# Second FFN stage: 20 products in another order, other stored weight sums, weights by order of use, and more of its start made ready in the first stage

## The chip, the cores and the metric

The kernel runs on one core of a Trainium2 chip. The metric is the device time of one execution in microseconds, from several runs; lower is better. One further execution was recorded by the profiler, and the profile and the trace come from it. The engines in them are PE (TensorE, matmuls), PEld (its weight loads), DVE (VectorE), ACT (ScalarE), POOL (GpSimd) and SP (SyncE, which here issues nearly all DMAs).

## The reference

Attention with a sigmoid in place of the softmax, for 8 batches of 12 heads, 448 positions and head size 64, then a feed-forward network with a leaky ReLU on all 3584 tokens (768 to 2048 to 768 features):

```python
scores = scale * np.matmul(q, k.transpose(0, 1, 3, 2)) - np.log(S)
attn = 1.0 / (1.0 + np.exp(-scores))
attn_out = np.matmul(attn, v)
x = attn_out.transpose(0, 2, 1, 3).reshape(B * S, H * D)
h = x @ w_in
g = np.maximum(0.01 * h, h)
out = g @ w_out
```

The values are float32 on the way in and out; the weights come as float64.

## The kernel before

**Precision.** A float32 operand is split into a high part, rounded by ScalarE (a cast), and a low part, the rest, subtracted by VectorE. A product of two such operands is three matmuls: high by high, high by low, low by high (`parts_mm`, L188, and the list at L976).

**Three stages.** First the attention. Beside it VectorE turns the float64 weights into float32 and makes the sums of weight blocks that the later stages use (`prep`, L342, with `firsts` and `second`); blocks and sums go to HBM. Then comes the first FFN stage (`First`, L629). It works on 4 quarters of the tokens (two batches of 448 each), and in each on 8 steps u with 7 products (a fast scheme for a 2 x 2 by 2 x 2 block product), a product being 9 matmuls of 128 x 448. Each u gives four blocks of g after the leaky ReLU. They are stored in HBM (`gd`), and so are sums of two of them that are named in `MADE` (L39), so that the second stage needn't make them.

**The second FFN stage.** In a quarter `w_out` is a grid of 3 x 4 blocks and g one of 4 x 2 blocks; the out grid has 3 x 2. Instead of 24 block products the kernel makes 20 (`PRODUCTS`, L42). A row of that table is: the weight form (a block or a sum of blocks, numbered by its place in HBM), the chain (A to E, an accumulator of two PSUM banks that goes on over several products), the operand ("21-30" is g block 21 less g block 30), and the reads of the accumulator that follow. "c10" copies the accumulator into output block 10 (ScalarE); "r", "+" and "-" combine it with a block already begun (VectorE: accumulator less block, block plus accumulator, block less accumulator); "!" says that the block is then complete, and it is stored. In the listing, products are counted from 0 in the order of the table.

A product has two halves, h = 0 and 1, each with half of the inner dimension. One half of one product is an item: 12 matmuls. There are 160 items, `items` (L787), 40 in each quarter. An item's operand is one of two kinds. If it lies in HBM as such (a raw block or a sum from `MADE`) it is one load, a cast and a subtraction. If not, two blocks are loaded, unless the product before has one of them, and VectorE first makes the sum, the tile gf (`Operand`, L800, steps `load`, `whole`, `high`, `low`).

All these tiles and the output blocks being built come from one list of 18 free buffers (12 in `gp`, 6 in `op`), first in, first out (`grab`, `drop`). A buffer goes back to the list when the instruction that ends its use has been issued; whoever gets it next waits on the chip until that use is over. The 6 of `op` join the list when the first FFN stage has been issued.

**The order of the work.** Every engine does its instructions in the order in which the program lists them; this order is written out by hand. In item k (`work`, L964) the program lists: the sum for item k+2 (for k+3 if it shares a block with a product that is itself a single load), the low part of k+1, the high part of k+2, the steps of the weight tiles that are due, the reads of the product that ended with item k-1 (L971), the 12 matmuls, the release of the item's operand, and then the loads (`g_load`, L881) of as many of the next items, up to 8 ahead, as the free list allows after the buffers that the next steps want (`wanted`, L869). A store is listed one item after the read that completes a block. All loads and stores go through SP, which waits at each of them until its buffer is free.

**Weights of the second stage.** 20 forms in 7 groups (`TRIPLES`, three forms each, the last with two) by 4 quarters of the inner dimension make 28 tiles (`Wide`, L165), each loaded, cast and split once. The first `AHEAD` = 7 of them are made ready in the last quarter of the first FFN stage (loop at L895, one every 6 products), the others during the first quarter of the second stage, one every 1.5 items. The same loop lists the first loads and steps of items 0 to 2 in the last five products of the first stage.

**Weights of the first stage.** They are staged, cast and split three and two products ahead (`advance`, L610), and in the last quarter a pool of 4 more staging buffers (L784) is there.

Of the kernel before, what the change touches and what calls it, by code (L numbers as in the profile page):

```python
# [25 lines left out]
AHEAD = 7  # L26
GG, OO, FAR = 12, 6, 8
# [11 lines left out]
MADE = {"01+30": "01", "00+30": "00", "10-21": "10", "21-20": "21", "11-10": "11", "11-21": "11"}  # L39
# [8 lines left out]
BLOCKS = "02", "01", "10", "00", "21", "03", "22", "11", "12", "13", "20", "23"  # L48
# [19 lines left out]
def attn_ffn_kernel(ctx: ExitStack, tc: tile.TileContext, qk, v, w_in, w_out, out):  # L68
# [245 lines left out]
    def second(u, dec):  # L314


        to = t2d[u // 2][:, u % 2]
        w = dec.rearrange("p a b -> p (a b)").rearrange("p (n m) -> p n m", m=P)
        dma(out=to[:, 7:8], in_=w[:, 0:1])
        dma(out=to[:, 10:17], in_=w[:, 1:8])  # L320
        s = block(F32, (12, P), f"ws1_{u}")

        def two(x, i, j):
            end = j + (1 if j > i else -1)
            return x[:, i:end if end >= 0 else None:j - i]

        def at(x, y):
            return two(w, BLOCKS.index(x), BLOCKS.index(y))

        for fn, to_, x, y in (  # L330
                (add, two(s, 8, 9), at("02", "03"), at("12", "13")), (sub, two(s, 10, 11), at("00", "03"), at("20", "23")),
                (sub, two(s, 1, 2), two(s, 9, 11), at("10", "22")), (add, two(s, 5, 6), two(s, 8, 10), at("11", "21")),
                (sub, two(s, 0, 4), at("10", "20"), at("13", "21")), (sub, two(s, 0, 4), two(s, 0, 4), two(s, 2, 1)),
                (sub, two(s, 3, 7), at("11", "01"), two(s, 2, 6)), (add, s[:, 3], s[:, 3], w[:, BLOCKS.index("12")]),
                (add, s[:, 7], s[:, 7], s[:, 5])):
            fn(to_, x, y)
            yield
        dma(out=to[:, :7], in_=s[:, :7])
        dma(out=to[:, 8:10], in_=s[:, 7:9])
        dma(out=to[:, 17:], in_=s[:, 9:])  # L340
# [443 lines left out]
    more = ExitStack()  # L784
    w1_stage.extend([more.enter_context(tc.tile_pool(name="stage2", bufs=4, side="right", reuse_waits="tile"))])
# [14 lines left out]
    class Operand:  # L800
# [4 lines left out]
        def __init__(self, k):  # L805
# [9 lines left out]
            self.lent, self.made, self.hi, self.ready = (), None, None, False  # L815
# [34 lines left out]
        def high(self):  # L850
            if self.hi is None:
                self.hi = grab(self.label("gh"))
            copy(out=self.hi, in_=self.x)

        def low(self):
            sub(self.lo, self.x, self.hi)
            if self.made is not None:
                drop(self.made)
# [10 lines left out]
    def wanted(k):  # L869
# [24 lines left out]

    for k in range(NOP, size):  # L895
        m, at = divmod(k - NOP, 6)
        if m < AHEAD:
            x = w2[use[m]]
            if at == 1:
                later(0, x.load)  # L900
                later(3, x.high)
                later(4, x.low)
        rest = size - k
        if rest <= 5:
            later(0, lambda r=rest: g_load(-r, 5 - r))
        for at, what in {2: ((0, "whole"), (0, "high")), 1: ((2, "whole"), (1, "whole"), (0, "low"), (1, "high"))}.get(rest, ()):
            later(0, lambda at=at, what=what: g_step(at, what))
        slot(first.step)
    while chores:
        slot()  # L910
    ps.close()
    more.close()
# [10 lines left out]
    psum = banks("ps_o", dict(acc=(4, 2)))  # L923
    firsts_at = {}
    for i, (_, chain, _, _) in enumerate(PRODUCTS):
        firsts_at.setdefault(chain, i)
    outs, accs = {}, {}
# [11 lines left out]
    def read(p, i):  # L939
        _, chain, _, reads = PRODUCTS[i]  # L940
        acc = accs[p, chain][:, :, :S]
        for x in reads:
# [8 lines left out]
            if x[3:]:  # L951
                later(1, lambda o=o: store(p, o))

    loads = {}
    for j in range(len(use) - AHEAD):
        loads.setdefault(j * 3 // 2, []).append(w2[use[AHEAD + j]])

    for k, (p, i, h) in enumerate(items):
        form, chain, _, reads = PRODUCTS[i]
        begins = h == 0 and firsts_at[chain] == i  # L960
        if begins:
            accs[p, chain] = psum("acc", f"acc{p}_{chain}")
        ending = k == len(items) - 1
        def work():  # L964
# [6 lines left out]
            if k % 2 == 0 and k:  # L971
                read(*items[k - 1][:2])
            me = operands[k]
            g = form // 3
            for m in range(2):
# [4 lines left out]
                if ending:  # L980
# [3 lines left out]
                    for cols, queue in zip(HALVES, (dma, dma_act)):  # L984
                        add(t[:, m, cols], t[:, m, cols], acc[:, m, cols])
# [51 lines left out]
```

## Time and profile before

| | |
|---|---|
| median of 3 runs | 1082.77 us (1082.52 to 1086.28) |
| profiled execution | 1081.94 us |
| its span, first to last instruction | 1080.1 us |
| mean granted TensorE clock | 0.993 |
| DMA bytes | 294.95 MB, 273 GB/s over the span |
| second FFN stage, first to last matmul | 658.46 to 1076.5 us |

How to read the rows: in a list of waits the numbers are microseconds in total, times, and the longest. A timeline row has start, duration, engine, line, operation, tiles and count, and in brackets the idle time before it with what ended it. A row of the chain has start, length, and engine or DMA. A group row has the busy time, the mean duration of one in ns, and the idle time before with what ended most of it. A DMA row has the KB of one transfer and the median from issue to landing. Nearly all instructions are issued through one helper, so they all have line 103, and the tile names tell them apart: px, py and pz are the first stage's accumulators, acc_A to acc_E those of the second; g is a loaded block (and later the low part), gf a sum made at run time, gh a high part, o an output block, w a weight tile, wx its staging tile.

### The profile page before, as it was taken

The numbers are of one execution on the slowest core, as the hardware profiler recorded it, in microseconds if no ns is written. First come the engines' busy times: TensorE is split into PE (matmuls) and PEld (weight loads), VectorE is DVE, ScalarE is ACT, GpSimd is POOL, SyncE is SP. The second block draws the span as 40 slices with busy tenths as digits, with TensorE's granted clock in tenths as the row PEclk, the third lists the DMA queues.
The fourth block names the chain that finished last, engine by engine and source line by source line (L and its number), as shares of the span: only waits on it lengthen the run. The fifth ranks groups of instructions, "written<-read, shape, count | busy, mean of one in ns | idle before, by whom it ended". The sixth has DMA issues, their size and how long they took to land.

```text
span 1080.1 us, 16340 instructions
## 1 busy us (share of the span) xinstructions
PE 1052.3 (97%) x5786; PEld 874.3 (81%) x5786; DVE 827.7 (77%) x1187; ACT 608.0 (56%) x829; POOL 0.3 (0%) x5
## 2 busy tenths in 40 slices
PE   9999999999999999999999999998999999999997
PEld 5555555558999998999899998987998899889977
DVE  5778889777897898789766566988767866786586
ACT  6877878876656655655565555754543344334432
POOL 0000000000000000000000000000000000000000
PEclk9999999999999999999999999999999999999999
DMA  7888888897889888998888789978946885697574
GB/s 260 275 289 274 288 296 271 278 330 224 269 264 334 258 279 265 301 338 277 284 246 272 251 277 363 356 266 307 341 157 222 304 315 194 196 339 266 188 249 159
DMA packets 126849, 294.95 MB, mean 273 GB/s; under 512 B 13360, under 2 KB 66608, under 8 KB 126768
## 3 DMA queue, kind: packets, MB, share of 16 engines
q1 hardware_dynamic: 126048, 293.23, 80.3%
q8 instruction: 45, 0.74, 0.3%
q10 hardware_dynamic: 720, 0.69, 0.2%
q14 instruction: 36, 0.29, 0.1%
HBM read 207.22 MB, written 86.64 MB: 272 GB/s over the span
## 4 chain that ended last, share of the span: by engine, by line
PE 80%; DVE 8%; DMA 8%; issue 2%; SPq 0%; ACT 0%; DVEq 0%; ACTq 0%
PE px_h L103 19%; PE pv L103 12%; PE sc L103 11%; PE acc_A L103 10%; PE pz_h L103 10%; PE acc_B L103 9%; PE py_h L103 5%; DMA out<-o 4%; DMA g<-g 3%; PE acc_C L103 3%; DVE g L103 2%; PE acc_D L103 2%; DVE gf L103 2%; DVE o L103 1%; DVE w L103 1%
## 5 line engine op out<-in xcount | busy, mean ns | idle before, releaser
L103 PE MATMUL px_h<-hi,w 128*128 128x448 f32 x768 | 231.8, 362 | 3.0 <-DVE w L103 3.0
L103 PEld LDWEIGHTS px_h<-hi,w 128*128 128x128 f32 x768 | 143.3, 187 | 16.3 <-DVE w L103 5.6
L103 PE MATMUL px_h<-lo,w 128*128 128x448 f32 x384 | 139.4, 363 | 0.0
L103 ACT ACTIVATE s<-sc 128x896 f32<-128x896 f32 x144 | 119.4, 933 | 9.4 <-PE sc L103 9.4
L103 ACT CAST gh<-gf 128x896 fp32r<-128x896 f32 x64 | 60.3, 942 | 112.0 <-DVE gf L103 100.4
L103 PE MATMUL pz_h<-hi,w 128*128 128x448 f32 x384 | 117.9, 361 | 0.0
L103 DVE TENSOR_TENSOR gf<-g,g 128x896 f32<-128x896 f32 x80 | 87.1, 1089 | 37.5 <-PE acc_A L103 16.1
L103 DVE TENSOR_TENSOR g<-g,gh 128x896 fp32r<-128x896 f32 x80 | 86.5, 1089 | 36.9 <-ACT gh L103 35.4
L103 DVE TENSOR_TENSOR w<-wx,w 128x768 fp32r<-128x768 f32 (+1 forms) x128 | 109.1, 853 | 6.2 <-ACT w L103 6.2
L103 PE MATMUL pv<-s,v 128*64 128x448 f32 x576 | 113.8, 543 | 0.0
L103 PE MATMUL acc_B<-gh,w 128*128 128x448 f32 x384 | 112.1, 362 | 0.0
L103 ACT CAST gh<-g 128x896 fp32r<-128x896 f32 x80 | 74.9, 942 | 54.5 <-PE acc_B L103 22.2
L103 PEld LDWEIGHTS sc<-qks 64*128 64x128 f32 x876 | 80.2, 188 | 23.8 <-issue 16.9
L103 ACT CAST w<-wx 128x768 fp32r<-128x768 f32 (+1 forms) x128 | 95.9, 750 | 0.7 <-DMA wx<-t 0.7
L103 PE MATMUL sc<-qks 64*128 64x448 f32 (+1 forms) x876 | 95.8, 369 | 0.2 <-ACT qks L103 0.2
L103 PE MATMUL acc_A<-gh,w 128*128 128x448 f32 x320 | 93.4, 362 | 0.0
L103 PEld LDWEIGHTS pv<-s,v 128*64 128x64 f32 x576 | 39.1, 137 | 63.3 <-issue 53.8
L103 ACT COPY c_h<-px_h 128x448 f32<-128x448 f32 x64 | 34.1, 533 | 89.5 <-PE px_h L103 80.3
L103 PE MATMUL acc_A<-g,w 128*128 128x448 f32 x256 | 78.1, 362 | 2.6 <-DVE g L103 2.6
L103 PEld LDWEIGHTS pz_h<-hi,w 128*128 128x128 f32 x384 | 71.9, 187 | 5.1
L103 PEld LDWEIGHTS acc_B<-gh,w 128*128 128x128 f32 x384 | 72.0, 187 | 4.9
L103 DVE TENSOR_TENSOR g<-gf,gh 128x896 fp32r<-128x896 f32 x64 | 69.4, 1086 | 8.5 <-ACT gh L103 8.5
(75 smaller groups left out, 1782.2 us busy)
## 6 DMA issues: line engine op xcount, KB each, us to landing
g<-g SPq DMA_DIRECT2D x200, 448.0 KB, 4.9
wx<-t SPq DMA_DIRECT2D x96, 384.0 KB, 4.5
g<-c_h SPq DMA_DIRECT2D x128, 224.0 KB, 4.5
g<-s SPq DMA_DIRECT2D x96, 224.0 KB, 4.5
qk<-in_qk SPq DMA_DIRECT2D x46, 448.0 KB, 5.3
wr<-in_w_in SPq DMA_DIRECT2D x32, 384.0 KB, 3.3
wr<-in_w_out SPq DMA_DIRECT2D x32, 384.0 KB, 3.8
out<-o SPq DMA_DIRECT2D x23, 448.0 KB, 5.1
```

What stands on the lines that cost most here:

```text
L103: return lambda *args, **kw: tc.keep_in_program_order(issue(*args, **kw))
```

## The change

- `PRODUCTS` has the same 20 kinds of products in another order, with other chains, and some sums have changed. `MADE` holds three other sums: 01-00, 20-10 and 31+01 in place of 00+30, 10-21 and 11-21. It is now a plain list.
- The weight forms lie in HBM in a new order (`FORM`), near the order of use; `second` writes them in seven pieces instead of five.
- The accumulators are four named pairs of banks, given out from a list that a chain joins again when its last read has been listed.
- `wanted` keeps two more buffers back (`SPARE`).
- Nine weight tiles (`AHEAD`) instead of seven are made ready in the first stage, one every 5 products, and those left are loaded one every 1.75 items. The four extra staging buffers are given up for the space.
- Items 0 to 3 are made ready wholly in the first stage, items 4 and 5 up to their sums, one step per product, ending two products before the stage's end (`READY`, `LEAD`).
- `advance` makes the first stage's weights ready one product earlier.
- The last read may add or subtract.

```diff
-AHEAD = 7
-GG, OO, FAR = 12, 6, 8
+AHEAD = 9
+GG, OO, FAR, SPARE = 12, 6, 8, 2
+READY, LEAD = 4, 2
...
-MADE = {"01+30": "01", "00+30": "00", "10-21": "10", "21-20": "21", "11-10": "11", "11-21": "11"}
+MADE = ("01+30", "01-00", "11-10", "20-10", "21-20", "31+01")
...
 PRODUCTS = (
-    (0, "A", "30", ("c10",)), (2, "B", "21-30", ("c21",)), (1, "A", "01+30", ("c11",)), (3, "B", "21", ("r11",)),
-    (4, "A", "01", ("r21",)), (5, "B", "10-21", ("c01",)), (6, "A", "10+01", ("c20",)), (7, "B", "21-20", ("c00",)),
-    (8, "A", "10", ("r00",)), (9, "B", "20-10", ()), (10, "A", "11-10", ("r01",)), (11, "B", "00+30", ("r10!",)),
-    (12, "D", "01-00", ("-00!",)), (13, "E", "11+01", ()), (14, "C", "30-31", ("-01!", "-21")), (15, "D", "30-20", ()),
-    (17, "C", "31+01", ()), (19, "E", "21-31", ("+21!",)), (18, "D", "10+00", ("-20!",)), (16, "C", "11-21", ("+11!",)))
-BLOCKS = "02", "01", "10", "00", "21", "03", "22", "11", "12", "13", "20", "23"
+    (0, "E", "11+01", ()), (1, "A", "30", ("c10",)), (2, "B", "21-30", ("c21",)), (3, "A", "01+30", ("c11",)),
+    (4, "E", "21-31", ("r21",)), (5, "C", "30-31", ("-21", "c01")), (7, "A", "01", ("+21!",)), (8, "B", "21", ("r11",)),
+    (6, "D", "01-00", ("c00",)), (9, "B", "10-21", ("+01",)), (10, "A", "10+01", ("c20",)), (11, "B", "21-20", ("+00",)),
+    (13, "A", "10", ("r00!",)), (12, "D", "30-20", ()), (14, "B", "20-10", ()), (15, "C", "31+01", ()),
+    (16, "D", "10+00", ("-20!",)), (17, "C", "11-21", ("+11!",)), (18, "B", "00+30", ("r10!",)), (19, "A", "11-10", ("r01!",)))
+FORM = ("21", "s0", "s2", "s1", "s11", "03", "00", "s4", "s3", "s5", "s6", "02", "22", "s7", "s8", "s9", "s10", "11", "10", "01")
+SUMS = tuple(x for x in FORM if x[0] == "s")
+BLOCKS = (*(x for x in FORM if x not in SUMS), "12", "13", "20", "23")
...
-        dma(out=to[:, 7:8], in_=w[:, 0:1])
-        dma(out=to[:, 10:17], in_=w[:, 1:8])
+        def keep(x, names, raw):
+            at = 0
+            for raw_, run in itertools.groupby(FORM, key=lambda name: name not in SUMS):
+                run = list(run)
+                if raw_ == raw:
+                    i = names.index(run[0])
+                    dma(out=to[:, at:at + len(run)], in_=x[:, i:i + len(run)])
+                at += len(run)
+
+        keep(w, BLOCKS, True)
...
-        while at_high < len(w1) and w1[at_high][0] <= t + 3:
+        while at_high < len(w1) and w1[at_high][0] <= t + 3 + (t >= 7):
...
-        while at_low < len(w1) and w1[at_low][0] <= t + 2:
+        while at_low < len(w1) and w1[at_low][0] <= t + 2 + (t >= 7):
...
-    w1_stage.extend([more.enter_context(tc.tile_pool(name="stage2", bufs=4, side="right", reuse_waits="tile"))])
...
         n += x.single or len([m for m in x.new if m not in x.lent]) < 2
+        n += SPARE
...
+    todo = []
+    for k in range(READY):
+        todo.append((k, "load"))
+    for k in range(READY):
+        todo += [(k + 2, "load")] * (k + 2 >= READY) + [(k, "whole"), (k, "high")]
+        todo += [(k + 2, "whole")] * bool(operands[k + 2].first()) + [(k, "low")]
+    ahead = READY + 2
+
     for k in range(NOP, size):
-        m, at = divmod(k - NOP, 6)
+        m, at = divmod(k - NOP, 5)
         if m < AHEAD:
             x = w2[use[m]]
-            if at == 1:
-                later(0, x.load)
-                later(3, x.high)
-                later(4, x.low)
-        rest = size - k
-        if rest <= 5:
-            later(0, lambda r=rest: g_load(-r, 5 - r))
-        for at, what in {2: ((0, "whole"), (0, "high")), 1: ((2, "whole"), (1, "whole"), (0, "low"), (1, "high"))}.get(rest, ()):
-            later(0, lambda at=at, what=what: g_step(at, what))
+            for n, what in ((0, "load"), (2, "high"), (3, "low")):
+                if at == n:
+                    later(0, getattr(x, what))
+        if k >= size - LEAD - len(todo) and todo:
+            later(0, lambda x=todo.pop(0): g_step(*x))
         slot(first.step)
...
-    psum = banks("ps_o", dict(acc=(4, 2)))
-    firsts_at = {}
+    psum = banks("ps_o", {f"acc{n}": (1, 2) for n in range(4)})
+    vacant, held = [3, 0, 1, 2], {}
+    firsts_at, lasts_at = {}, {}
...
+        if i == lasts_at[chain]:
+            vacant.append(held.pop((p, chain)))
...
-        loads.setdefault(j * 3 // 2, []).append(w2[use[AHEAD + j]])
+        loads.setdefault(j * 7 // 4, []).append(w2[use[AHEAD + j]])
...
+            if begins:
+                held[p, chain] = vacant.pop(0)
+                accs[p, chain] = psum(f"acc{held[p, chain]}", f"acc_{chain}{p}")
...
-                        add(t[:, m, cols], t[:, m, cols], acc[:, m, cols])
+                        x, y = (t, acc) if reads[0][0] in "+-" else (acc, t)
+                        (add if reads[0][0] == "+" else sub)(t[:, m, cols], x[:, m, cols], y[:, m, cols])
```

`high` and `low` of an operand now return at once if they were done before.

More of the change, by code (lines that the diff above doesn't have):

```diff
@@ L1 @@
+import itertools
 import math
@@ L328, in at, with sums, one @@
             return two(w, BLOCKS.index(x), BLOCKS.index(y))
+        def sums(i, j):
+            return two(s, SUMS.index(f"s{i}"), SUMS.index(f"s{j}"))
+        def one(i):
+            return s[:, SUMS.index(f"s{i}")]
         for fn, to_, x, y in (
[L331 to L335, printed above, removed]
+                (add, sums(8, 9), at("02", "03"), at("12", "13")), (sub, sums(10, 11), at("00", "03"), at("20", "23")),
+                (sub, sums(1, 2), sums(9, 11), at("10", "22")), (add, sums(5, 6), sums(8, 10), at("11", "21")),
+                (sub, sums(0, 4), at("10", "20"), at("13", "21")), (sub, sums(0, 4), sums(0, 4), sums(2, 1)),
+                (sub, sums(3, 7), at("11", "01"), sums(2, 6)), (add, one(3), one(3), w[:, BLOCKS.index("12")]),
+                (add, one(7), one(7), one(5))):
             fn(to_, x, y)
             yield
-        dma(out=to[:, :7], in_=s[:, :7])
-        dma(out=to[:, 8:10], in_=s[:, 7:9])
-        dma(out=to[:, 17:], in_=s[:, 9:])
+        keep(s, SUMS, False)
     def prep():
@@ L814, in __init__ @@
             self.new = [n for n in self.names if n not in self.shared]
-            self.lent, self.made, self.hi, self.ready = (), None, None, False
+            self.lent, self.made, self.hi = (), None, None
+            self.ready = self.has_high = self.has_low = False
             if self.before:
@@ L850, in high @@
         def high(self):
+            if self.has_high:
+                return
+            self.has_high = True
             if self.hi is None:
@@ L855, in low @@
         def low(self):
+            if self.has_low:
+                return
+            self.has_low = True
             sub(self.lo, self.x, self.hi)
@@ L893, in attn_ffn_kernel @@
     w2 = {(g, u): Wide(g, u, t2a, "t2") for g, u in use[:AHEAD]}
+    todo = []
[5 more added lines that the diff above has]
+    ahead = READY + 2
     for k in range(NOP, size):
-        m, at = divmod(k - NOP, 6)
+        m, at = divmod(k - NOP, 5)
         if m < AHEAD:
             x = w2[use[m]]
-            if at == 1:
-                later(0, x.load)
-                later(3, x.high)
-                later(4, x.low)
-        rest = size - k
-        if rest <= 5:
-            later(0, lambda r=rest: g_load(-r, 5 - r))
-        for at, what in {2: ((0, "whole"), (0, "high")), 1: ((2, "whole"), (1, "whole"), (0, "low"), (1, "high"))}.get(rest, ()):
-            later(0, lambda at=at, what=what: g_step(at, what))
+            for n, what in ((0, "load"), (2, "high"), (3, "low")):
[3 more added lines that the diff above has]
+            later(0, lambda x=todo.pop(0): g_step(*x))
         slot(first.step)
+    assert not todo
     while chores:
@@ L911, in attn_ffn_kernel @@
     ps.close()
-    more.close()
     left.close()
@@ L922, in attn_ffn_kernel @@
         w2[g, u] = Wide(g, u, pool, tag, KQ if small else None)
-    psum = banks("ps_o", dict(acc=(4, 2)))
-    firsts_at = {}
+    psum = banks("ps_o", {f"acc{n}": (1, 2) for n in range(4)})
+    vacant, held = [3, 0, 1, 2], {}
+    firsts_at, lasts_at = {}, {}
     for i, (_, chain, _, _) in enumerate(PRODUCTS):
         firsts_at.setdefault(chain, i)
+        lasts_at[chain] = i
     outs, accs = {}, {}
@@ L960, in attn_ffn_kernel @@
         begins = h == 0 and firsts_at[chain] == i
-        if begins:
-            accs[p, chain] = psum("acc", f"acc{p}_{chain}")
         ending = k == len(items) - 1
```

1 line of the change is left out of this document (removed).

## The prediction

> **What bounds the kernel now.** I read the page's engine line first, then PE's waits by stage, then the chain that ended last, then the timeline of one stall.
>
> ```profile
> PE 1052.3 (97%) x5786; PEld 874.3 (81%) x5786; DVE 827.7 (77%) x1187; ACT 608.0 (56%) x829; POOL 0.3 (0%) x5
> ...
> PE px_h L103 <- DVE w L103: 3.0, 6, 1.3
> ...
> PE acc_C L103 <- DVE g L103: 12.7, 9, 2.2
> PE acc_A L103 <- DVE g L103: 2.6, 2, 1.6
> PE acc_C L103 <- DVE o L103: 1.0, 2, 0.8
> ```
>
> TensorE is the bound, and no matmul is removed, so only what it loses can be won. The waits are few and have one form: it wants an operand (g) that VectorE hasn't finished; the 3.0 us on w are in the first FFN stage. But they don't give the whole loss; the timeline does.
>
> ```profile
> 658.46 0.37 PE L103 MATMUL acc_A<-gh,w 128*128 128x448 f32 x1
> 659.82 0.47 PE L103 MATMUL acc_A<-g,w 128*128 128x448 f32 x1 [0.99 <-DVE g L103]
> 664.09 0.47 PE L103 MATMUL acc_A<-g,w 128*128 128x448 f32 x1 [1.59 <-DVE g L103]
> ...
> 767.65 4.80 PE acc_A L103 x24
> 869.77 4.80 PE acc_A L103 x24
> 972.55 4.80 PE acc_A L103 x24
> ...
> 1075.02 0.47 PE L103 MATMUL acc_C<-gh,w 128*128 128x448 f32 x1 [0.78 <-DVE o L103]
> 1076.13 0.37 PE L103 MATMUL acc_C<-gh,w 128*128 128x448 f32 x1
> ```
>
> A product (counted from 0) is 24 matmuls in 4.80 us, 0.20 each; an item, its half, is 2.4. The stage has 4 quarters of 20 products, 1920 matmuls, 384.0 us. It runs from 658.46 to 1076.13 + 0.2: 417.9 us, so **33.9 us are lost**. The quarters begin at 658.46, 767.65, 869.77 and 972.55 (the chain counts from 0.16 inside) and take 109, 102.1, 102.8 and 103.9 where 96.0 would do. The start rows cost 0.99 + 1.59, and about 0.28 more each for the pipe (below): 3.1. The last wait costs 0.78 + 0.28 = 1.06. The other 29.7 lie late in the quarters; here is the stall of the second one.
>
> ```profile
> 835.54 0.37 PE L103 MATMUL acc_C<-gh,w 128*128 128x448 f32 x1
> 838.01 0.47 PE L103 MATMUL acc_C<-g,w 128*128 128x448 f32 x1 [2.10 <-DVE g L103]
> ...
> 839.79 0.95 PE L103 MATMUL acc_C<-gh,w 128*128 128x448 f32 x2
> 840.54 0.58 PE L103 MATMUL acc_C<-g,w 128*128 128x448 f32 x1
> ...
> 833.08 1.08 DVE L103 TENSOR_TENSOR o<-o,acc_D 128x896 f32<-128x896 f32 x1
> 835.86 1.09 DVE L103 TENSOR_TENSOR gf<-g,g 128x896 f32<-128x896 f32 x1 [1.69 <-DMA g<-g]
> 836.87 1.08 DVE L103 TENSOR_TENSOR g<-gf,gh 128x896 fp32r<-128x896 f32 x1
> ...
> 828.74 0.39 SPq L103 DMA_DIRECT2D out<-o  x1
> 834.19 0.39 SPq L103 DMA_DIRECT2D out<-o  x1
> ...
> 834.19 6.13 DMA out<-o
> 840.39 3.31 DMA g<-g
> 846.95 6.44 DMA out<-o
> ```
>
> Start to start is 2.47 us, so the wait of 2.10 costs 2.27, and 0.1 more behind it: hence my 0.28. Then matmuls come every 0.373 us (839.79, two, 840.54) for about ten: another 1.7. TensorE waits for a low part (836.87) that stands on VectorE behind the sum gf of the next item (835.86), which waited for its load. By the code that load takes the buffer of an output block whose store was issued just before (828.74), so it waits on the sync queue until the store has landed, with all loads and stores behind it. The chain shows the same link: store 6.13, load 3.31, store 6.44. In the old order six output blocks hold 6 of 18 buffers from product 7 to 11, and seven of the last eight products need a sum made at run time.
>
> **The change part by part.** Durations:
>
> ```profile
> L103 DVE TENSOR_TENSOR gf<-g,g 128x896 f32<-128x896 f32 x80 | 87.1, 1089 | 37.5 <-PE acc_A L103 16.1
> L103 ACT CAST gh<-g 128x896 fp32r<-128x896 f32 x80 | 74.9, 942 | 54.5 <-PE acc_B L103 22.2
> L103 DVE TENSOR_TENSOR w<-w 128x768 fp32r<-128x768 f32 (+1 forms) x28 | 25.6, 915 | 5.7 <-ACT w L103 5.6
> ...
> g<-g SPq DMA_DIRECT2D x200, 448.0 KB, 4.9
> wx<-t SPq DMA_DIRECT2D x96, 384.0 KB, 4.5
> out<-o SPq DMA_DIRECT2D x23, 448.0 KB, 5.1
> ...
> DMA to landing us min/median/max: 1.7/4.7/7.4
> ...
> 738.45 7.11 DMA g<-g
> ```
>
> *Order of products.* Ten products of twenty still need a run-time sum, 17 reads of accumulators stay 17, 11 of them on VectorE. Loads rise from 25 to 27 per quarter and half: 16 more in all, of 4.9 us to landing, beside TensorE as long as they come early. What moves is where they crowd. I followed the free buffers through both orders: the old one falls to 4 items loaded ahead at product 11, and by the same count as below the load above is some 6 us late; in the new one at most five blocks are held, and at least 5 items are ahead. Its tightest places, with store 6.13 and load 4.9:
> - Product 17's load takes the block stored after product 12. From the start of item 26: the store goes out at +1.9 (0.4 for the last matmul's end, 1.09 for the read, 0.4 for the queue), has landed at +8.0, and the load at +12.9. Its sum must be done before the low part of item 33 (+16.8 less 2.2 and 0.1): due +14.5. 1.6 us to spare.
> - At the quarter's end four stores in a row each hold up the load behind: 1.9 + 4 x 6.5 + 4.9 = +32.8 from item 34, due +33.7 (item 49, +36.0, less 2.3). 0.9 us to spare.
> - ScalarE's cast for product 9 takes the block stored after product 6: 1.9 + 5.1 + 0.94 + 1.09 + 0.2 = +9.2, due +9.6; with 6.13 it is 0.65 late.
>
> So I take 0.65 per quarter for the second to fourth, 2.0 us, between 0 and the rival's price below.
>
> *Two spare buffers kept back (SPARE)* and four accumulators in an order of their own cost no instruction; none of the four is taken again before its last read is 6 items old.
>
> *Four items and nine weight tiles in the first stage.* The start loss of 3.1 goes. Added there: six operations of 1.09 and two weight halves of 0.915 on VectorE, 8.4 us; on ScalarE about 3.5.
>
> ```profile
> 354.00:455.00 101.00, 99.85 (x498) 92.76 (x497) 86.95 (x141) 57.57 (x93) 0.00 (x0) 1.00 0.86 276
> ...
> 619.00:640.00 21.00, 21.00 (x107) 19.68 (x106) 14.20 (x21) 11.43 (x21) 0.00 (x0) 1.00 0.91 295
> 640.00:658.40 18.40, 18.40 (x94) 17.25 (x93) 10.85 (x16) 10.04 (x17) 0.00 (x0) 1.00 0.89 313
> ...
> 658.00:768.00 110.00, 101.61 (x487) 91.25 (x486) 95.03 (x99) 58.28 (x70) 0.00 (x0) 0.98 0.90 328
> 768.00:870.00 102.00, 98.92 (x481) 90.76 (x480) 73.32 (x71) 41.10 (x45) 0.00 (x0) 0.98 0.72 249
> ```
>
> (Columns: stretch, length, busy PE, PEld, DVE, ACT, POOL, clock, DMA share, GB/s.) VectorE is busy 25 of the last 39.4 us of that stage; 33.4 would be 85%, as in 354 to 455. So it fits without loss if the weights keep their lead. The item loads go out three to four products (5.4 to 7.2 us) before their use against 4.9 to landing; if one is late, VectorE stands, and the weights' low parts behind it: at most 2 us, 0 taken.
>
> *The first quarter* keeps 19 weight tiles instead of 21. VectorE had 95.0 us there in 110; without 8.4 it is 86.6 in 96. Issued back to back its operations are 1.00 apart (835.86, 836.87): a product with a sum and a read takes 5.0, and 1.0 of weights makes it 6.0 against 4.8. Six such products (4, 5, 9, 16, 17, 18) overrun by 7.2 us; lighter ones (6 to 8, 11, 12, 14, 15) stand between. Between 0 and 7.2 I take 2.5, nearer to hidden, for these lighter ones.
>
> *Weights of the first stage one product earlier.* The six waits on w cost 3.0 + 6 x 0.28 = 4.7. The longest is 1.3, and one product is 1.8: nearly all goes. The cast now comes four products (7.2 us) after the load instead of five, against 4.5 to landing; ScalarE will sometimes wait, which is still no later than before. 0.7 stays (0 to 2.5): gain 4.0. Three run-time sums per u instead of 2 or 4, and 7 stores of weight blocks per u for 5, lie beside TensorE.
>
> **Sum.** Second stage left: 2.5 + 2.0 + 1.06 = 5.6, gain 28.3; first stage 4.0. The profiled execution took 1081.94 (span 1080.1): 1081.94 - 32.3 = 1049.6. The median of the runs is 0.8 above it: **1050**.
>
> On the half rate, the Trainium skill (TensorE: Matmul & The Clock Gate, Part 1) says that the clock drops after an idle window of about 3.4 us. Here it dropped after 2.10 us, so the trace disagrees and I count 1.7 us with each gap of that size; by the page the first rival below would end at 1055. On stores, the Trainium skill (DMA: Bandwidth & Descriptors, Anatomy of one DMA) gives about 2.0 us plus bytes over 436 GB/s on the GpSimd path, as an estimate 3.1 us for 448 KB; this trace's stores, from the sync engine, have a median of 5.1, which decides. With 3.1 both store rivals below would vanish.
>
> **Rivals.**
> 1. *A stall is left in each quarter*, at ScalarE's cast for product 9. It decides above a store of 5.5 us. At 7.4 TensorE waits 1.9, and the clock drop adds 1.7: 3.6 instead of 0.65 three times, and 3.6 in the first quarter, 12.4 in all: 1062. For it: stores of 6.13 and 6.44 above. Against: few loads go out beside that store.
> 2. *The loss stays per quarter*, because sums and reads crowd VectorE, not buffers: 6.1 in each, 25.5 with the last wait: gain 8.4 + 4.0, 1069.5. Against: VectorE is busy 73 of 102 in the second quarter, and its long wait was for a load.
> 3. *Slower: the sync queue falls behind.* All stores at 7.4 and loads at 7.11 (the chain's row at 738.45): the quarter's end is 1.9 + 4 x 7.8 + 7.1 - 33.7 = 6.5 late, 8.2 with the clock, three times; product 17 is 1.9 late, 3.6 with the clock, four times: 39 us, 1088.6. With stores of 7.4 it eats up the gain from loads of some 6.9 us on. Against: DMA is busy 0.72 in the second quarter, and 8% more loads don't fill it.
> 4. *It does nothing*: the new stalls add up to the old ones; nothing in the rows points there.
>
> **How the numbers follow.** Forecast, 1045 to 1056, 0.63; rival 1, to 1063, 0.20; rival 2, 0.08; rival 3, 0.05; rival 4, 0.02; below 1045, 0.02 (with no loss but the last wait and nothing left in the first stage it is 1044.4). The range from 1045 to 1063 takes in the forecast and rival 1. Within 0.5% (5.4 us, about what a measurement of this kernel can tell from no change) only rival 4 falls: faster 0.93, same 0.02, slower 0.05.
>
> **What would show it.** Right: PE's waits on g near 3 us, none at the start, quarters of 96 to 97 us with the first up to 99, no px_h waits on w, clock 1.00 throughout. Wrong: ScalarE's gh waiting on out stores with TensorE behind (rival 1); sums waiting on PE or other sums, not on loads (2); loads on the sync queue waiting for stores at each quarter's end (3); new waits in 619 to 658.

## The result and the profile after

The changed kernel takes **1054.76 us** (median of 4 runs, 1053.16 to 1056.98), the kernel before, run beside it, 1083.25 us (1082.52 to 1086.28): ratio 0.973, interval 0.971 to 0.976, 28.5 us faster. Forecast were 1050, with a range of 1045 to 1063. The profiled execution took 1055.2 us with a span of 1053.4.

From the page of the kernel after: the engines' busy time, and two rows of the DMA issues.

```profile
PE 1041.1 (99%) x5786; PEld 871.4 (83%) x5786; DVE 827.4 (79%) x1187; ACT 607.0 (58%) x829; POOL 0.3 (0%) x5
...
g<-g SPq DMA_DIRECT2D x216, 448.0 KB, 5.3
...
out<-o SPq DMA_DIRECT2D x23, 448.0 KB, 4.8
```

The work is the same: 5786 matmuls, 1187 VectorE instructions, 829 on ScalarE, and 16 item loads more, as counted. TensorE's busy time fell by 11 us with the same matmuls: 5.7 us of that are 33 matmuls of the second stage that came 0.373 us apart before, at half rate, which counts as busy. There are none now.

The windows of the kernel after, around the four quarters of the second stage (length; busy PE, PEld, DVE, ACT, POOL; clock; DMA share; GB/s):

```profile
660.00:760.00 100.00, 97.31 (x482) 89.64 (x481) 84.41 (x88) 54.43 (x66) 0.00 (x0) 1.00 0.96 344
760.00:856.00 96.00, 96.00 (x482) 90.04 (x481) 73.81 (x72) 42.13 (x47) 0.00 (x0) 1.00 0.83 282
856.00:952.00 96.00, 96.00 (x482) 89.94 (x481) 73.16 (x72) 41.69 (x46) 0.00 (x0) 1.00 0.85 286
952.00:1050.00 98.00, 97.00 (x484) 90.19 (x482) 71.23 (x71) 39.46 (x44) 0.00 (x0) 1.00 0.76 263
```

The second and third quarter have no loss left: 96.00 us, all of it matmuls. What remains is in the first quarter, where DMA is at 0.96, and in the last product. PE's waits in the kernel after, total, times and longest:

```profile
PE pz_h L107 <- ACT c_h L107: 1.2, 3, 0.7
...
PE px_h L107 <- DVE c_h L107: 1.0, 3, 0.5
...
PE acc_C L107 <- DVE g L107: 1.0, 1, 1.0
PE acc_B L107 <- DVE g L107: 0.9, 1, 0.9
PE acc_A L107 <- DVE o L107: 0.8, 1, 0.8
PE px_h L107 <- ACT c_h L107: 0.6, 2, 0.4
PE acc_A L107 <- ACT o L107: 0.4, 1, 0.4
PE acc_E L107 <- DVE g L107: 0.4, 1, 0.4
```

The waits on g, 12.7 and 2.6 us for two accumulators alone, are down to 2.3 us in three waits, and no wait on w is left. But the first FFN stage (px_h, pz_h) has not become free of waits: where it waited for weights, it now waits for c_h, evictions of its accumulators, which are listed behind weight steps on ScalarE and VectorE.

For a balance I take a stage's **loss**: from the start of its first matmul to that of the next stage's first (in the second FFN stage to the last matmul's start and 0.2), less 0.20 us for each of its matmuls, 2016 in the first FFN stage and 1920 in the second. In brackets are the quarters; each has 504 or 480 matmuls.

| us | start of the first FFN stage | loss, first FFN stage | loss, second FFN stage | span |
|---|---|---|---|---|
| before | 250.3 | 5.0 [1.1, 1.8, 2.1, 0.0] | 33.9 [13.0, 6.1, 6.8, 8.0] | 1080.1 |
| after | 251.5 | 5.7 [1.4, 2.5, 1.3, 0.5] | 5.2 [4.0, 0.0, 0.0, 1.1] | 1053.4 |

The span fell by 26.7: 28.7 from the second stage, less 0.8 lost in the first and 1.2 in the attention. The attention's code is the same in both, and with unchanged attention the kernels below begin their first FFN stage anywhere from 250.1 to 251.6, so this last is a difference between executions.

### The profile page after: what moved, and what is told of

It is laid out like the page before. It is cut to its first block, busy times and chain, and to the rows that moved or that the text cites. A ratio compares the mean times of both kernels' runs of the same rounds, so it can differ in the third digit from the quotient of the medians.

```text
span 1053.4 us, 16409 instructions
## 1 busy us (share of the span) xinstructions
PE 1041.1 (99%) x5786; PEld 871.4 (83%) x5786; DVE 827.4 (79%) x1187; ACT 607.0 (58%) x829; POOL 0.3 (0%) x5
## 4 chain that ended last, share of the span: by engine, by line
PE 89%; DVE 4%; DMA 3%; issue 1%; ACT 1%; SPq 1%; ACTq 0%; DVEq 0%
PE px_h L107 19%; PE pv L107 12%; PE acc_B L107 10%; PE sc L107 10%; PE acc_A L107 10%; PE pz_h L107 9%; PE acc_D L107 5%; PE acc_C L107 5%; PE py_h L107 4%; PE acc_E L107 3%; DVE w L107 1%; SPq L107 1%; DMA g<-c_h 1%; DMA w<-t 1%; DVE wd L107 1%
## 5 line engine op out<-in xcount | busy, mean ns | idle before, releaser
L107 PE MATMUL acc_A<-gh,w 128*128 128x448 f32 x384 | 112.0, 362 | 1.2 <-DVE o L107 0.8
L107 PE MATMUL acc_B<-gh,w 128*128 128x448 f32 x320 | 93.0, 362 | 0.0
L107 ACT CAST g<-gf 128x896 fp32r<-128x896 f32 x40 | 37.8, 945 | 75.8 <-DVE gf L107 71.3
L107 PE MATMUL acc_B<-g,w 128*128 128x448 f32 x256 | 78.3, 363 | 0.9 <-DVE g L107 0.9
L107 PEld LDWEIGHTS acc_A<-gh,w 128*128 128x128 f32 x384 | 72.0, 188 | 6.6 <-DVE o L107 1.2
L107 PEld LDWEIGHTS px_h<-lo,w 128*128 128x128 f32 x384 | 72.0, 188 | 4.8
L107 DVE SCALAR_TENSOR_TENSOR wd<-wr,wd 128x384 int32<-128x384 int32 x128 | 71.3, 557 | 3.4
```

The source lines that it names most:

```text
L107: return lambda *args, **kw: tc.keep_in_program_order(issue(*args, **kw))
```

## The experiments

The same balance for all of them; the ratio is to the kernel before, run on the same chip, with its 95% interval. All but the second and fourth start from the kernel after.

| kernel | loss, first FFN stage | loss, second FFN stage | median us | ratio |
|---|---|---|---|---|
| order only (e3) | 6.3 [1.8, 2.6, 1.9, 0.0] | 7.4 [5.6, 0.6, 0.2, 1.1] | 1057.52 | 0.977 (0.975 to 0.978) |
| start only (e4) | 8.3 [1.1, 1.8, 2.2, 3.3] | 32.2 [12.2, 6.9, 6.0, 7.2] | 1084.08 | 1.001 (1.000 to 1.002) |
| weights not earlier (e1) | 11.1 [1.8, 2.6, 1.9, 4.8] | 5.3 [4.2, 0.0, 0.0, 1.1] | 1059.03 | 0.978 (0.976 to 0.980) |
| before, three blocks not stored (e2) | 5.4 | 20.2 [10.1, 4.0, 2.6, 3.5] | 1069.05 | 0.988 (0.986 to 0.990) |
| no spare buffers (e5) | 6.0 [1.0, 2.5, 1.3, 1.2] | 14.9 [8.7, 1.3, 2.3, 2.6] | 1065.33 | 0.984 (0.982 to 0.985) |
| two buffers fewer (e7) | 5.8 [0.8, 2.5, 1.3, 1.1] | 34.1 [11.8, 10.8, 8.3, 3.2] | 1084.22 | 1.002 (1.000 to 1.003) |
| tiles cast later (e10) | 6.3 [1.8, 2.6, 1.9, 0.0] | 5.6 [4.2, 0.0, 0.0, 1.4] | 1057.05 | 0.974 (0.971 to 0.977) |
| five stored sums (e11) | 3.6 [0.7, 1.5, 1.4, 0.0] | 9.7 [6.5, 0.0, 2.1, 1.1] | 1056.58 | 0.975 (0.973 to 0.977) |
| load earlier (e6) | 6.4 [0.7, 2.5, 1.3, 1.8] | 3.5 [2.5, 0.0, 0.0, 1.1] | 1054.71 | 0.974 (0.972 to 0.975) |
| weights' pace (e8) | 6.1 [1.0, 2.5, 1.3, 1.3] | 4.6 [2.3, 0.0, 0.9, 1.5] | 1053.50 | 0.973 (0.971 to 0.975) |
| combined (e9) | 5.2 [0.7, 2.5, 2.0, 0.0] | 1.7 [0.6, 0.0, 0.0, 1.1] | 1050.72 | 0.968 (0.965 to 0.970) |

### Which part of the change brings the time

**The order alone.** The products, sums, forms, accumulators and SPARE of the kernel after, with the start and the first stage's weights of the kernel before:

```diff
-AHEAD = 9
+AHEAD = 7
...
-        while at_high < len(w1) and w1[at_high][0] <= t + 3 + (t >= 7):
+        while at_high < len(w1) and w1[at_high][0] <= t + 3:
...
+    w1_stage.extend([more.enter_context(tc.tile_pool(name="stage2", bufs=4, side="right", reuse_waits="tile"))])
...
-        m, at = divmod(k - NOP, 5)
+        m, at = divmod(k - NOP, 6)
...
+        rest = size - k
+        if rest <= 5:
+            later(0, lambda r=rest: g_load(-r, 5 - r))
...
-        loads.setdefault(j * 7 // 4, []).append(w2[use[AHEAD + j]])
+        loads.setdefault(j * 3 // 2, []).append(w2[use[AHEAD + j]])
```

> The new kernel without its start: seven weight tiles, the old steps before the second stage, the old pace of the weights, and the first stage's weights as before. Theory A (order of products gives the late losses back, the start gives only the first quarter): quarters two to four lose 0, 0 and 1.1 us as in the new kernel, the first 8 to 12; total 1058 to 1064. Rival (the lead of the start is what carries the new order): quarters two to four lose 2 us or more each.

The second stage loses 7.4 instead of 33.9: 26.4 of the change's 28.7 us are the order's, together with its stored sums, accumulators and SPARE. The first quarter loses 5.6, less than the 8 to 12 expected; 5.2 of it lie in its first two products, where the kernel after loses nothing.

**The start alone.** The reverse: the old order with nine weight tiles and four items made ready, and no `stage2` pool.

```diff
-AHEAD = 7
+AHEAD = 9
+READY, LEAD = 4, 2
...
-        m, at = divmod(k - NOP, 6)
+        m, at = divmod(k - NOP, 5)
...
+            for n, what in ((0, "load"), (2, "high"), (3, "low")):
+                if at == n:
+                    later(0, getattr(x, what))
+        if k >= size - LEAD - len(todo) and todo:
+            later(0, lambda x=todo.pop(0): g_step(*x))
```

> The old kernel with the new start alone: nine weight tiles and four items ready in the first stage, the rest of the weights at the new pace; old order, old sums, no spare buffers. Theory A: the first quarter loses 7 to 10 us instead of 13, the other three 6 to 8 each as before; total 1077 to 1080. Rival (start carries all): the later quarters improve too, total below 1070.

It brings nothing: 1.001 (1.000 to 1.002). The two waits at the stage's start are gone, but the first quarter loses 12.2 instead of 13.0 (7 to 10 were expected), and the last quarter of the first FFN stage loses 3.3 where it lost nothing. What is given back there, and by what, the next run shows.

**The first stage's weights not earlier.** Only this undone in the kernel after:

```diff
-        while at_high < len(w1) and w1[at_high][0] <= t + 3 + (t >= 7):
+        while at_high < len(w1) and w1[at_high][0] <= t + 3:
...
-        while at_low < len(w1) and w1[at_low][0] <= t + 2 + (t >= 7):
+        while at_low < len(w1) and w1[at_low][0] <= t + 2:
```

> The new kernel with the first FFN stage's weights cast and split three and two products ahead again. What is at stake: that stage loses 4.95 us before and 5.71 after, where 0.7 was forecast. Theory A (waits traded): moving the weights forward puts them ahead of the evictions c_h on ScalarE and VectorE, so the waits on w come back here and the waits on c_h go; the stage loses 4 to 6 us, the total moves by less than 1.5 us. Theory B (the lead is worth its 4 us, and something else in the change costs 4 us there): the w waits come on top of the c_h waits, the stage loses 9 to 10 us, the total 1059.

The first FFN stage then loses 11.1 instead of 5.7. So the earlier weights are worth 5.4, but only 1.1 of that lies in the first three quarters (6.3 to 5.2), which they were forecast to clear. 4.3 lies in the last, where the kernel before lost nothing. Three more kernels below (e5, e7, e8) have the first FFN stage of the kernel after unchanged, and lose 4.6 to 4.8 in its first three quarters and 1.1 to 1.3 in the last; so the two shares are 1.1 to 1.7 and 3.5 to 4.3. The timeline of this kernel there (start, duration, engine, operation; in brackets the idle time before and what ended it):

```profile
635.06 0.83 ACT L107 CAST w<-w 128x768 fp32r<-128x768 f32 x1 [4.45 <-DMA w<-t]
635.79 0.93 ACT L107 CAST g<-gf 128x896 fp32r<-128x896 f32 x1
636.63 0.83 ACT L107 CAST w<-wx 128x768 fp32r<-128x768 f32 x1
637.37 0.57 ACT L107 ACTIVATE c_h<-c_h 128x448 f32<-128x448 f32 x1
637.51 0.47 PE L107 MATMUL px_h<-hi,w 128*128 128x448 f32 x1 [2.07 <-ACT w L107]
```

ScalarE stands 4.45 us at the cast of a second-stage weight tile whose load has not landed. Behind it stand the cast of a first-stage weight tile (636.63), for which TensorE waits 2.07, and evictions. The changed start casts the tile two products after its load; before it was three. So the start made a new stall, and the earlier weights mostly cover it.

### What made the old stall

**The old order with fewer stores.** The kernel before, but blocks 10, 00 and 01 are not stored:

```diff
+        if o not in ("10", "00", "01"):
+            dma(out=place(p, o).rearrange("m p s -> p m s"), in_=t)
-        dma(out=place(p, o).rearrange("m p s -> p m s"), in_=t)
```

> The old kernel, in which the output blocks 10, 00 and 01 are computed but not stored (9 to 12 of the stores left out), so that the loads which take their buffers wait for VectorE's last read instead of a store's landing. Theory A (loads held behind stores on the sync queue cause the late losses): the second stage's quarters lose 1 to 3 us instead of 6 to 8, the total falls by 12 to 18 us. Theory B (sums and reads crowd VectorE): the quarters still lose 5 to 7 us, the total falls by less than 4.

The second stage's loss falls from 33.9 to 20.2. 5.7 of the 13.7 us is the half rate, which doesn't come any more. The quarters still lose 10.1, 4.0, 2.6 and 3.5, where theory A put 1 to 3 for each. In the waits of the second stage one sees what went. VectorE's waits there before:

```profile
DVE gf L103 <- DMA g<-g: 12.6, 12, 2.1
```

and with the stores left out, VectorE's and PE's:

```profile
DVE gf L103 <- DMA g<-g: 0.8, 2, 0.6
```

```profile
PE acc_C L103 <- DVE g L103: 6.7, 9, 1.5
...
PE acc_A L103 <- DVE g L103: 2.9, 3, 1.6
```

VectorE practically no longer waits for loads. Loads behind stores, with the half rate that followed, made about 14 of the 33.9 us. Most of the rest is not late loads: TensorE still waits 6.7 + 2.9 us for low parts while loads are in time. In the old order seven of the last eight products need a sum, beside reads on the same engine. In this run's trace VectorE has eight operations in a row, 1.0 us apart, from 839.54 on, and TensorE waits 0.9 us for a low part at 845.69, in the midst of them; the same wait comes at 944.27 and 1042.75. That agrees with VectorE's crowding, but no run takes the sums or reads away.

**Two buffers fewer.** If the new order has its gain from buffers, it must lose it with fewer of them; if it were the spread of VectorE's work, it would keep most.

```diff
-GG, OO, FAR, SPARE = 12, 6, 8, 2
+GG, OO, FAR, SPARE = 12, 4, 8, 2
```

> The new kernel with 16 buffers instead of 18. Theory A (buffers, through the time at which loads can go out, set the late losses): the list falls to 3 or 4 items ahead in products 8 to 16, several loads come up to one item late, quarters two to four lose 2 to 5 us each, total 1062 to 1075. Rival (VectorE's sums and reads set them): those quarters stay below 1 us, total below 1058.

The whole gain is gone: 34.1 us of loss in the second stage, 1084.22, more than the 1062 to 1075 expected. The new order needs its buffers; its margin is less than two. This doesn't say that the old order lacked buffers; that rests on the run before. VectorE's waits in this kernel:

```profile
DVE gf L107 <- DMA out<-o: 21.1, 3, 8.1
```

These three stand where the first three quarters end, the place of the prediction's third rival: 21.0 of the 34.1 us lie in the last product of these quarters. 28 matmuls of the stage are at half rate, 4.9 us.

**No buffers kept back.** The prediction said of SPARE only that it costs no instruction.

```diff
-GG, OO, FAR, SPARE = 12, 6, 8, 2
+GG, OO, FAR, SPARE = 12, 6, 8, 0
```

> The new kernel with SPARE = 0: the same buffers, but two more are given to loads early, and what takes a buffer gets one that was given back more recently. Theory A (the new order holds fewer blocks, which is enough): quarters two to four lose under 1 us more in all, total within 2 us of the new kernel. Rival (the two buffers kept back are what keeps waits out): they lose 2 us or more each, total above 1060.

This costs 10 us (second stage 5.2 to 14.9): the theory that the spare buffers carry next to nothing is wrong. The waits of VectorE say how:

```profile
DVE gf L107 <- DMA out<-o: 12.2, 4, 3.3
```

With no buffer kept back, the loads use up the list, and the next run-time sum gets the block that has just been stored, so VectorE itself waits until the store has landed. 4.6 of the 9.7 us lie at products 8 and 9, where these four waits stand and the kernel after loses nothing; what makes the rest wasn't taken apart. With two kept back that wait falls to ScalarE's cast for product 9, which is where the prediction put it (its first rival). From the waits and the timeline of the kernel after:

```profile
ACT gh L107 <- DMA out<-o: 18.7, 4, 5.0
```

```profile
795.39 0.40 SPq L107 DMA_DIRECT2D out<-o  x1
...
799.62 0.95 ACT L107 CAST gh<-gf 128x896 fp32r<-128x896 f32 x1 [4.59 <-DMA out<-o]
...
801.08 1.09 DVE L107 TENSOR_TENSOR g<-gf,gh 128x896 fp32r<-128x896 f32 x1
...
803.68 0.36 PE L107 MATMUL acc_B<-gh,w 128*128 128x448 f32 x1
```

ScalarE waits 18.7 us here, once a quarter, and TensorE not at all: the store went out at 795.39 and had landed 4.2 us later, so the low part is done at 802.17, and its item begins at 803.68. The rival needed a store above 5.5.

### The first FFN stage

**Tiles cast later.** As "weights not earlier", but the second-stage tiles are cast four and split five products after their load.

```diff
-            for n, what in ((0, "load"), (2, "high"), (3, "low")):
-                if at == n:
-                    later(0, getattr(x, what))
+            if at == 0:
+                later(0, x.load)
+                later(4, x.high)
+                later(5, x.low)
```

> The kernel of the first experiment (first stage's weights not earlier), in which the second stage's weight tiles made ready in the first stage are cast four products after their load and split after five, instead of two and three. In the first experiment the first stage's last quarter loses 4.8 us. Theory A (the cast stands on ScalarE waiting 4.5 us for its load, with evictions and the first stage's casts behind): that quarter loses under 1.5 us, total 1054.5 to 1056.5. Rival (the work added on VectorE and ScalarE is what costs it): it still loses 4 us or more, total 1058 to 1060.

The last quarter's loss goes from 4.8 to 0.0, and the span from 1057.6 to 1053.5. So the stall is the tile's cast, not the amount of work that the start adds to this quarter, nor the four staging buffers, which this kernel lacks too. (The medians, 1059.03 and 1057.05, lie closer together, with intervals that just meet; the place of the loss is what decides.)

The first three quarters still lose 6.3, as in e1 and e3 (6.31, 6.31 and 6.32), where the kernel before lost 4.95. The three share the new `MADE` and `FORM` and have the old lead of the weights; e4, with the old `MADE` and `FORM`, loses 5.0. So one of these two, or both, cost 1.4 there. `MADE` stores as many sums as before (96 in all), but at other steps. `FORM` raises the stores of weight blocks from 25 to 35 in these quarters, since the weights' preparation, which begins beside the attention, goes on in them. No run separates the two.

**One stored sum less.** 31+01 is taken from `MADE`, and made at run time in the second stage; the rest as in the run before.

```diff
-MADE = ("01+30", "01-00", "11-10", "20-10", "21-20", "31+01")
+MADE = ("01+30", "01-00", "11-10", "20-10", "21-20")
```

> The kernel of the tiles cast later (first stage's weights not earlier), with 31+01 no longer made and stored in the first stage: two sums for each u from 0 to 3 instead of three, and one more sum at run time in each quarter of the second stage. Without the earlier weights the first stage's first three quarters lose 6.3 us in three runs, against 5.0 in the old kernel, and their longest waits stand at u = 2 and 3, where the old ones stand at u = 5. Theory A (the stored sums crowd VectorE where they are made): these quarters lose 3 to 4.5 us. Rival (the seven stores per u, or anything else): they still lose 6 us or more. The second stage pays 2 to 10 us for it, so the total is at or above 1057.

The first FFN stage falls from 6.3 to 3.6, and the second rises from 5.6 to 9.7. So stored sums do not lie beside TensorE for nothing. This one costs 2.7 there and saves 4.1 here, but the ratios of the two kernels, 0.975 and 0.974, can't be told apart.

Why the earlier weights clear so little of this is in the timeline of the kernel after, on VectorE and PE:

```profile
501.04 1.16 DVE L107 TENSOR_TENSOR s<-c_h,c_h 128x448 f32<-128x448 f32 x2
502.12 1.55 DVE L107 TENSOR_TENSOR s<-x,x 128x1344 f32<-128x1344 f32 x1
...
504.32 1.42 DVE L107 TENSOR_TENSOR w<-wx,w 128x384 fp32r<-128x384 f32 x2
505.66 0.62 DVE L107 TENSOR_TENSOR c_h<-c_h,px_h 128x448 f32<-128x448 f32 x1
...
506.33 0.47 PE L107 MATMUL px_h<-hi,w 128*128 128x448 f32 x1 [0.51 <-DVE c_h L107]
```

Two stored sums, a sum for the operands, two steps of the weights' preparation (left out here) and two weight splits stand in a row, and the eviction that frees px_h comes last. With the splits listed earlier the weight is ready, but the eviction is late: TensorE waits at the same crowd for another tile.

**Loads one product earlier, too.** If the casts, now one product earlier, wait for loads and hold up the evictions, earlier loads would help.

```diff
-        while at_load < len(w1) and w1[at_load][0] <= t + 8 and at_load < at_low + len(w1_stage):
+        while at_load < len(w1) and w1[at_load][0] <= t + 8 + (t >= 7) and at_load < at_low + len(w1_stage):
```

> The new kernel in which the first stage's weight loads go out one product earlier too, so that five products lie again between load and cast. In the new kernel ScalarE waits 8.3 us for these loads, with evictions (c_h) behind, and the stage's first three quarters lose 5.2 us. Theory A (the casts that wait for loads delay the evictions): ScalarE's wait for wx falls below 3 us, those quarters lose 2 to 3.5 us, total 1051 to 1053. Theory B (the weights' split, listed earlier on VectorE, delays the evictions by itself): they still lose 4.5 to 5.5 us, total within 1 us of the new kernel.

ScalarE's waits for wx fall from 8.3 to 4.8 us, yet the second and third quarter lose exactly what they lost (2.53, 1.29). The first loses 0.7 instead of 1.4 and the last 1.8 instead of 0.5, but e5, e7 and e8, with the first stage of the kernel after, lose 0.8 to 1.0 and 1.1 to 1.3 there: most of these two differences lies between executions. The time is that of the kernel after, 0.974 (0.972 to 0.975) to 0.973 (0.971 to 0.976). So in the second and third quarter it is not late loads, which fits the row of VectorE's work above.

### The first quarter of the second stage

**The pace of the weights.** The 19 tiles left, one every 1.5 items instead of 1.75:

```diff
-        loads.setdefault(j * 7 // 4, []).append(w2[use[AHEAD + j]])
+        loads.setdefault(j * 3 // 2, []).append(w2[use[AHEAD + j]])
```

> The new kernel with the remaining 19 weight tiles loaded one every 1.5 items, as before, instead of 1.75. In the new kernel's first quarter (4.0 us lost) two waits of 0.95 stand at products 17 and 18, whose loads come out behind a store while weights are still loaded; two of 0.4 stand early, where ScalarE's weight casts wait for their loads with a copy of an output block behind. Theory A: weights end four items earlier, the two late waits go, the early ones grow by up to 1.5 us; quarter one 2 to 4 us, total 1052 to 1055. Rival (the early crowd is worse than the late one): quarter one 5 us or more, total above 1056.

The first quarter loses 2.3 instead of 4.0. The total, 1053.50 with 0.973 (0.971 to 0.975), can't be told from the kernel after; 0.9 us are lost in the third quarter instead. Nor is the pace alone shown to be the cause: e6, whose second stage is the kernel after's, loses 2.5 in this quarter, with one late wait of 0.4 in place of two of about 0.95. What went are the two late waits, which these rows of the timeline of the kernel after show, behind the two early ones:

```profile
672.92 0.83 ACT L107 CAST w<-w 128x768 fp32r<-128x768 f32 x1 [6.53 <-DMA w<-t]
...
674.51 0.89 ACT L107 COPY o<-acc_A 128x896 f32<-128x896 f32 x1
...
727.19 0.39 SPq L107 DMA_DIRECT2D out<-o  x1
...
732.31 0.80 SPq L107 DMA_DIRECT2D g<-g  x2
...
736.64 8.00 SPq L107 DMA_DIRECT2D g<-g  x8
...
745.21 1.09 DVE L107 TENSOR_TENSOR gf<-g,g 128x896 f32<-128x896 f32 x1 [1.65 <-DMA g<-g]
...
747.36 2.48 PE L107 MATMUL acc_C<-g,w 128*128 128x448 f32 x11 [0.95 <-DVE g L107]
...
750.96 1.28 PE L107 MATMUL acc_B<-g,w 128*128 128x448 f32 x5 [0.93 <-DVE g L107]
```

Late: the load that takes the buffer of the block stored at 727.19 goes out at 732.31, when that store has landed. It is the load of product 17, the place that the prediction named as the tightest, and by itself it is in time. But SP has stood still before it, and what follows goes out in a crowd: of the eight loads issued from 736.64 on, the DMA rows of the stretch from 736 to 746 say

```profile
g<-g SPq DMA_DIRECT2D x8, 448.0 KB, 7.5
```

The sum at 745.21 waits 1.65 for one of them, and TensorE 0.95 for the low part behind it, and 0.93 more before VectorE has caught up. In the kernel after it happens in this quarter alone, where the weights' loads come on top. Early: ScalarE waits 6.5 us for a weight tile's load, and the copy that frees acc_A (674.51) stands behind that cast; PE's waits for o at acc_A (0.4) and for g at acc_E (0.4) are there.

**All of it together.** The kernel after with later tile casts, earlier loads in the first stage and the faster pace, and in the second stage the weights cast three and split four items after their load:

```diff
-            for far, step in ((3, "low"), (2, "high"), (0, "load")):
+            for far, step in ((4, "low"), (3, "high"), (0, "load")):
```

> An attempt at a better version: the new kernel with the tile casts of the first stage four products after their load, first-stage weight loads one product earlier, the rest of the weight tiles one every 1.5 items, their casts three items after the load instead of two. If the waits add up as the single runs say, the first stage loses 4.5 to 5 us (last quarter near 0), the second 1.1 to 2.5 us, total 1050 to 1052. If every such wait is only replaced by the next one, the total stays at 1053 to 1055.

1050.72 us (1049.43 to 1051.10), 0.968 (0.965 to 0.970): faster than both kernels, and its interval does not reach that of the kernel after (0.971 to 0.976). The second stage loses 1.7, of which 1.1 are the last product's wait for its block. PE's waits in it:

```profile
PE pz_h L107 <- ACT c_h L107: 1.6, 4, 0.7
PE px_h L107 <- DVE c_h L107: 1.0, 3, 0.5
...
PE acc_A L107 <- DVE o L107: 0.8, 1, 0.8
...
PE acc_A L107 <- ACT o L107: 0.2, 1, 0.2
```

No wait on g is left. What each of the four edits brings of this wasn't taken apart, beyond the runs above.

## Why the prediction was right, and where not

The gain was forecast as 32.3 of the profiled execution, 1081.94 to 1049.6. It was 26.7, and the profiled execution took 1055.2. The 5.6 between are 4.8 from the first FFN stage and 1.2 from the attention, less 0.4 that the second stage brought beyond its forecast.

- **Second stage, 33.9 to 5.6: right in sum**, 5.2, and partly by luck: the first quarter took 1.5 more than its term, the later ones 2.0 less, 0.0 each where 0.65 was put; the last wait 1.1, as said. That the old loss came from loads behind stores is borne out for about 14 of 33.9 (e2). Some 16 more, beside the start and the last wait, stayed with loads in time; there VectorE's crowding, which the prediction set aside as its second rival, is the likely cause. The new order moves sums and reads apart as well as buffers, so the gain came either way; no run says how much by which.
- **The first quarter, 2.5: too little**, 4.0. The reason was partly another: I priced VectorE's crowding, but the waits are for loads in a quarter with DMA at 0.96, on ScalarE and SP. The late half (2.4) of it begins at product 17's load, the place named as the tightest.
- **"Nearly all goes" of the first stage's w waits, gain 4.0: this step failed.** The stage lost 0.8 more instead. Three things were missed. The steps of the weights that come earlier are listed ahead of evictions, and those are then late (the w waits became c_h waits). "Three run-time sums per u instead of 2 or 4, and 7 stores of weight blocks per u for 5, lie beside TensorE" was wrong: one of the two, or both, cost 1.4 there. And the tile's cast came only two products after its load, which stands in the diff and got no price; it would have cost 4.8, of which the earlier weights covered 3.5 to 4.3.
- **The added start, "0 taken", at most 2 us**: with the earlier weights 0.5 to 1.3 in the last quarter, within the bound; without them 4.8, beyond it. "ScalarE will sometimes wait, which is still no later than before" is the sentence that hid it: what stands behind the waiting cast on ScalarE was not looked at.
- **The start loss of 3.1 goes: right only for the waits.** In the kernel with the start alone the first quarter improved by 0.8, and with the order there by 1.5 (5.6 to 4.0).
- **SPARE "cost no instruction"** is true and was no answer: it moves a wait from VectorE to ScalarE, and without it 10 us are lost, about half of them there.
- **Rivals.** The first had the right place: ScalarE waited there, without TensorE. Its threshold of 5.5 us wasn't tried; the four stores there landed in 4.1 to 4.6. The second (VectorE crowded, 6.1 left in each quarter) is out for the new order: the later quarters lose nothing. The third (stalls at each quarter's end) did not come: the stores before product 17's load took 4.4 to 5.1 us, not 7.4, and a crowd of loads with a median of 7.5 came in the first quarter alone. With two buffers fewer (e7) the quarters' ends did stall.

## What to carry to other kernels

When operands and results share one list of buffers, follow which instruction gets the buffer that a store still holds: the same wait was free on ScalarE, which had slack, and cost some 5 us on VectorE, which feeds TensorE, and two buffers can decide the whole gain. A step moved ahead is priced by what then stands behind it on its in-order engine: keep a cast of loaded data as far behind its load as the slowest load takes. Setting it behind the evictions that free accumulators might do as well; that wasn't tried. Work moved from a stalled stage into a full one is not won until the full one has been counted again.

## What the runs showed of the hardware

**The half rate goes by windows of time, not by the length of the gap.** The prediction counted 1.7 us with each gap of 2.10 us. It came after 2.10 us in the kernel before, and after 6.11 us in e7. It did not come after 2.75 us in e3, 2.07 in e1, 2.05 in e4 and 1.84 in e11. The granted clock shows why. In the kernel before it is 0.50 in four stretches of 3.41 us inside the second stage, which start at 747.04, 839.20, 941.60 and 1044.00: 27, 30 and 30 times 3.413 us apart. In all thirteen traces of this case the clock changes lie whole multiples of 3.413 us apart, so each execution can be cut into windows of this length. Here are the second of these stretches with the window ahead of it, and windows around the gap of 2.75 in e3 and that of 2.05 in e4 (columns as above):

```profile
835.79:839.20 3.41, 1.31 (x7) 1.12 (x7) 3.31 (x4) 0.95 (x2) 0.00 (x0) 1.00 0.94 284
839.20:842.61 3.41, 3.41 (x11) 3.05 (x10) 1.96 (x3) 0.93 (x1) 0.00 (x0) 0.50 0.77 271
```

```profile
669.31:672.72 3.41, 1.57 (x8) 1.12 (x6) 1.33 (x2) 0.23 (x1) 0.00 (x0) 1.00 0.96 335
672.72:676.14 3.42, 2.51 (x12) 2.36 (x13) 3.42 (x4) 0.71 (x1) 0.00 (x0) 1.00 1.02 393
```

```profile
942.50:945.92 3.42, 2.00 (x10) 1.88 (x11) 3.38 (x4) 1.76 (x2) 0.00 (x0) 1.00 0.92 316
```

In the two FFN stages of the thirteen traces there are eight windows at the full clock in which TensorE was busy at most 1.52 of 3.41 us. The half rate followed each of them, for one window, or for two in e7. It followed none of the others, which have 1.57 us or more. So a gap of 2.10 us inside one window lowers the clock, and one of 2.75 that lies across two does not. That the share of busy time decides is inferred from these windows; no run shifted a gap on purpose. The Trainium skill (TensorE: Matmul & The Clock Gate, Part 1) says that the clock is gated by a window of about 3.4 us that runs freely. These traces show a window of that length, and gaps of nearly one length ending differently agree with its running freely. That it takes about 3.4 us of idle time does not agree: TensorE was busy for up to 1.52 us of the window ahead of a drop.

**A transfer of 448 KB has no one duration.** Item loads in the kernel after had a median of 5.3 us over the whole execution and of 7.5 in the crowded stretch above, with DMA at 0.96 in that quarter. The price that decides a tight place is the one of its own stretch.
